# A gated mix of segment attention and a feed-forward network: row maxima from high halves in four 32-row tiles, and the network in one pass

## The chip, the cores and the metric

The kernel runs on one core of a Trainium2 chip. The metric is the device time of one execution in microseconds; the median of three runs of the kernel before is 552.74 us (552.01 to 553.68). The core has TensorE (PE, matmuls, results in PSUM), VectorE (DVE), ScalarE (ACT), GpSimd (POOL) and SyncE (SP), which here issues all DMAs. PSUM has eight banks of 128 x 512 floats.

## The reference

From the same x (2048 x 448) come an attention result a and a feed-forward result b; the output is g a + (1 - g) b, with g a sigmoid of x times a gate vector. The sequence falls into N = 4 segments of L = 512, with H = 16 heads of Dh = 28.

```python
logits = einsum("bhqd,bhkd->bhqk", qs, ks) * scale + mask     # causal, within a segment
a_dot = einsum("bhqk,bhkd->bhqd", softmax(logits), vs)
a_mem = (phi(qs) @ M) / (phi(qs) @ z + 1e-6)                  # memory of earlier segments
o = sigmoid(beta) * a_mem + (1 - sigmoid(beta)) * a_dot
M, z = M + phi(ks)^T vs, z + sum(phi(ks))
a = o @ wo
b = silu(x @ w1) @ w2                                         # 448 -> 1792 -> 448
```

Inputs are float32. The kernel reaches that accuracy with pairs of 16-bit numbers: every operand is split into a high and a low half (`halves`: one ScalarE copy, one subtraction), and a product is the sum of three matmuls: high by high, high by low and low by high.

## The kernel before, in words

**Stage one** (`project`) makes Q, K and V of every segment, the gates, and the memory part of attention. Q and K are made for a group of four heads at a time (112 of 128 rows; the 16 others carry a slice of the 14th block of w1, so that its x @ w1 comes along). With 4 segments and 4 groups there are 16 groups t. The halves of Q, K and V go out to DRAM and come back in another layout: a tile of `ring` holds for four heads 84 rows, the halves (high, low, high) of Q beside (high, high, low) of K, and two rows more for the negative row maximum.

**Row maxima** (`maxima`, L620): softmax wants a maximum for each row before the exponentials. For a group of heads TensorE multiplies the 84 rows of Q and K again, row block by row block (i = 0 to 3, with 128 (i+1) columns, causal), into banks "sc". For i = 0 a matmul with a mask (L640) goes ahead, and one VectorE instruction reduces four heads; the rest is masked and reduced by VectorE at once (L654). The maxima are transposed, split in halves, sent through DRAM and put into the two extra rows of `ring` as a term of the score product, lifted by 8 ln 2.

**Attention** (`attention`, L1160): for each head three score tiles, keys by queries (L1182), exponentials on ScalarE (L1187), two GpSimd instructions that zero what is not causal (L1190, L1193), the high half on ScalarE (L1199) and the low half in three GpSimd subtractions (L1203), then P times V with a column of ones for the denominators (L1216, into "cc") and the sum on VectorE (L1224). At the end of a group the result is scaled and stored to `o_scr`.

**The network** (`unit`, L1051) works in two passes over w1's 14 blocks of 128 columns: blocks 0 to 9 for all four segments, then 10 to 13. For a segment, each block gives a 128 x 512 tile of x @ w1 (11 matmuls by `product`, L540), the activation (ScalarE, VectorE, ScalarE, VectorE: L1063 to L1069), and the tile in halves in one of 12 buffers `ghl`. Then for each of four 128-token blocks the second product sums over the pass's blocks (three matmuls of 448 columns for each block, L1086). The first pass leaves partial sums in `p_scr` (`part`); the second takes them back. All blocks of w1 and w2 are loaded once in stage one to find their sizes, and again before their use; five blocks of w1 are converted at the end of stage one, the rest of the first pass's at the start of attention, the second pass's between the passes.

**The output** (`last_part`, L1280) belongs to the second pass: the attention result of a token block is loaded, the memory part added (GpSimd), split, transposed by DMA, multiplied by wo (11 matmuls of 448 columns), and added to both parts of the network's result in two VectorE instructions.

**What sets the order.** `Sched` is a planner that runs while the program is built: every piece of work is a task with an engine, a cost in microseconds, dependencies, buffers and a priority number; it walks in modelled time, gives each engine the task that can begin first and, among equals, that of the lowest priority, and so writes out a fixed order for every engine, SP's queue too. Attention's priorities are 10 per head (0 to 640), the first pass's are spread from -69 to 870. PSUM banks are rings: "mm" 4, "sc" 3, "cc" 1 after stage one. A task that takes a buffer waits until the one that many places earlier is used up. Constants at the top shift priorities of single kinds of work.

The line numbers named are those of the kernel before.

## Time and profile before

| | |
|---|---|
| median of 3 runs | 552.74 us (552.01 to 553.68) |
| profiled execution, its own time | 553.39 us |
| its span, first to last instruction | 551.7 us |
| mean granted TensorE clock | 0.984 |
| TensorE, VectorE, ScalarE, GpSimd busy | 534.8, 409.3, 391.8, 354.7 us |
| moved by DMA | 81.68 MB, mean 148 GB/s |

A busy share is a mean over stages. Matmuls are pipelined and the end of each is modelled, so that neighbours overlap in the record and the sum of durations is more than what the stream takes; the distance from one start to the next is what counts. A group of instructions shows its count, its busy time, the mean duration of one in ns, and the idle time of the engine just before them with the releaser. The chain of waits goes back from the last instruction to what released it each time.

### The profile page before, as it was taken

What the parts mean: (1) busy time and instruction counts of PE and PEld (TensorE: products, weight loads), DVE (VectorE), ACT (ScalarE), POOL (GpSimd) and SP (SyncE); (2) the same over time, 40 slices, a digit from 0 to 9 for tenths busy, and PEclk for the clock granted to TensorE, in tenths of its full rate; (3) what the DMA queues carried; (4) which work ended last, traced back from release to release, by engine and by line L of the source; (5) the groups of instructions that cost most, each with busy time, mean ns of one, the idle gap of its engine ahead of it and who ended that gap; (6) DMA issues with size and microseconds to landing.
All of it is one profiled execution on the core that took longest, in us unless ns stands there. A gap on an engine that the chain in (4) does not pass through costs nothing.

```text
span 551.7 us, 11563 instructions
## 1 busy us (share of the span) xinstructions
PE 534.8 (97%) x4009; PEld 294.7 (53%) x4009; DVE 409.3 (74%) x1074; ACT 391.8 (71%) x688; POOL 354.7 (64%) x519
## 2 busy tenths in 40 slices
PE   4699999999999999999999999999999999999997
...
PEclk8689999999999999999999999999999999999999
...
GB/s 276 205 175 227 203 236 233 225 226 166 170 233 162 146 100 137 87 42 80 121 102 102 58 98 124 121 103 112 100 18 53 138 49 152 219 241 212 225 160 83
DMA packets 89194, 81.68 MB, mean 148 GB/s; under 512 B 55176, under 2 KB 78856, under 8 KB 89136
## 3 DMA queue, kind: packets, MB, share of 16 engines
...
q14 instruction: 27, 0.22, 0.1%
...
## 4 chain that ended last, share of the span: by engine, by line
PE 89%; DVE 4%; DMA 4%; ACT 1%; issue 1%; SPq 0%; DVEq 0%; ACTq 0%
PE mm L540 31%; PE mm L1086 23%; PE sc L540 12%; PE sc L1182 6%; PE sc L644 6%; PE cc L1216 6%; DMA rawf<-in_w_dram 2%; PE cc L932 1%; DMA xraw<-in_x_dram 1%; PE cc L895 1%; DVE sizes L388 1%; DVE sc L654 1%; DMA v_scr<-vt 1%; PE sc L640 1%; PE cc L933 0%
## 5 line engine op out<-in xcount | busy, mean ns | idle before, releaser
L1203 POOL TENSOR_TENSOR phl<-pf,phl 128x384 f16<-128x384 f32 (+1 forms) x192 | 189.5, 1008 | 16.2 <-ACT phl L1199 16.2
L1086 PE MATMUL mm<-wb,ghl 128*128 128x448 f16 (+1 forms) x684 | 148.8, 349 | 0.0
L540 PE MATMUL mm<-xh,wa 128*128 128x512 f16 x572 | 141.4, 379 | 0.0
L1187 ACT ACTIVATE pf<-sc,es 128x512 f32<-128x512 f32 (+1 forms) x192 | 109.7, 623 | 19.8 <-PE sc L1182 18.6
L654 DVE CUSTOM_DVE_ANT_0 sc<-sc,mk 128x384 f32<-128x384 f32 (+1 forms) x192 | 104.8, 572 | 20.4 <-PE sc L644 19.1
L1086 PEld LDWEIGHTS <-ghl 128*128 128x128 f16 x684 | 65.0, 97 | 52.5 <-DVE ghl L508 0.3
L1199 ACT ACTIVATE phl<-pf 128x1280 f16<-128x1280 f32 x64 | 81.3, 1277 | 14.9 <-POOL pf L1193 14.9
L540 PEld LDWEIGHTS <-wa 128*128 128x128 f16 x572 | 53.6, 97 | 54.4 <-issue 1.4
L1182 PE MATMUL sc<-ring 86*128 86x512 f16 (+3 forms) x256 | 59.3, 299 | 0.4 <-ACT pf L1187 0.2
L644 PE MATMUL sc<-ring 84*128 84x128 f16 (+3 forms) x256 | 58.2, 299 | 0.1
L1224 DVE TENSOR_REDUCE oraw<-cc 128x116 f32<-128x232 f32 x64 | 25.3, 395 | 30.8 <-PE cc L1216 30.6
L1063 ACT ACTIVATE th<-mm,ths 128x512 f32<-128x512 f32 x52 | 35.8, 699 | 16.0 <-PE mm L540 15.8
L1216 PEld LDWEIGHTS <-phl 128*128 128x128 f16 x1280 | 41.9, 96 | 9.1
L540 PE MATMUL mm<-xh,wqs 128*128 128x512 f16 x176 | 44.5, 390 | 1.0 <-ACT wqs L516 0.7
L551 POOL TENSOR_TENSOR ol<-ol,ml 128x448 f32<-128x448 f32 x12 | 13.7, 1138 | 48.7 <-DMA ol<-o_scr 37.2
L1065 DVE SCALAR_TENSOR_TENSOR mm<-th,mm 128x512 f32<-128x512 f32 x52 | 35.7, 694 | 10.9 <-ACT th L1063 10.9
L1216 PE MATMUL cc<-vg,phl 128*128 128x29 f16 (+1 forms) x1280 | 43.6, 182 | 0.0
L540 PE MATMUL sc<-wvs,xh 128*128 128x450 f16 x176 | 39.9, 368 | 3.1 <-ACT wvs L516 2.1
L540 PE MATMUL mm<-xh,wks 128*128 128x512 f16 x176 | 42.1, 380 | 0.0
L1069 DVE SCALAR_TENSOR_TENSOR ghl<-mm,ghl 128x512 f16<-128x512 f32 x52 | 35.1, 683 | 5.6 <-ACT ghl L1067 5.2
L1182 PEld LDWEIGHTS <-ring 86*128 86x128 f16 x256 | 23.8, 97 | 22.0 <-issue 1.1
L1067 ACT ACTIVATE ghl<-mm 128x512 f16<-128x512 f32 x52 | 30.9, 604 | 6.5 <-DVE mm L1065 6.4
(165 smaller groups left out, 835.9 us busy)
## 6 DMA issues: line engine op xcount, KB each, us to landing
...
```

What stands on the lines that cost most here:

```text
L540: nc.tensor.matmul(ps(), *p[i], start=(i == 0), stop=(i == n - 1))
L644: nc.tensor.matmul(ps.v[:, u:u + n], rg.v[:KS, 0, hh, i * 128:(i + 1) * 128], rg.v[:KS, 1, hh, :n], start=(i > 0), stop=(i > 0 or j == 3), ...
L654: nc.vector.tensor_tensor_reduce(r, r, MK[:, L - n:], 1.0, NEG, OP.add, OP.max, mx.v[:, hh, i:i + 1])
L1063: e1 = sact(L, lambda ps=ps, th=th: nc.scalar.activation(th.v, ps.v, AF.Tanh, scale=ths[:, s:s + 1]), m, DER[s], takes=[th], uses=[ps], pr ...
L1065: e2 = dve(L, lambda ps=ps, th=th: nc.vector.scalar_tensor_tensor(ps.v, th.v, 1.0, ps.v, op0=OP.add, op1=OP.mult), e1, uses=[ps, th], prio=p0)
L1069: e4 = dve(L, lambda ps=ps, g=g: nc.vector.scalar_tensor_tensor(g.v[:, 1], ps.v, DOWN, g.v[:, 0], op0=OP.mult, op1=OP.subtract), e3, uses= ...
L1086: nc.tensor.matmul(ps.v[:, lo:hi], g.v[:, y, sl], w.v[:, z, lo:hi], start=(j == 0 and i == 0), stop=(j == len(fs) - 1 and i == 2))
L1182: nc.tensor.matmul(ps.v[:, e:e + w], rg.v[:KK, 1, hh, j * 128:(j + 1) * 128], rg.v[:KK, 0, hh, j * 128:], start=True, stop=True)
L1187: ex.append(sact(e, lambda b=b, ps=ps, pf=pf, e=e: nc.scalar.activation(pf.v[:, b, :e], ps.v[:, :e], AF.Exp, scale=es[:, s:s + 1]), m, *ex ...
L1199: hi = copy(1280, lambda hl=hl, flat=flat: nc.scalar.activation(hl.v[:, 0], flat(), AF.Copy), *mk, takes=[hl], uses=[pf], prio=p0 + 2)
L1203: low = pool(w - u, lambda hl=hl, flat=flat, u=u, w=w: nc.gpsimd.tensor_sub(hl.v[:, 1, u:w], flat()[:, u:w], hl.v[:, 0, u:w]), low, uses=[ ...
L1216: nc.tensor.matmul(p[:, i, :2 - z], hl.v[:, z, u:u + 128], vg.v[:, j, hh, :2 - z], start=(z == zs[0] and i == 0), stop=(z == zs[-1] and j ...
```

## The change

1. *Row maxima from the high halves alone, four heads at once.* The scratch tensors of Q and K become one per segment, stored in one DMA of 128 rows. Beside `ring`, a tile `hq` is loaded with the high halves of Q and K: head h lies in rows 32 h to 32 h + 27. Three steps of matmuls take four heads each, every head in its own 32 rows of the array and its own bank ("sc", "sc", "sc", "cc"); the planner treats a step as one task that takes four banks, costs it as one head's columns and a constant (`SWITCH`), and holds back other tasks for these banks when it is due. The matmul with the mask is gone, and VectorE masks and reduces every block of every head. The maximum of high halves is not the exact maximum; the lift becomes 6 ln 2.
2. *A guard.* The whole kernel becomes `mix`. After attention it checks that the reciprocals of all denominators lie between 1/60000 and 1/32 and sets a flag. At the end, if the flag is set, a second copy of the program runs with exact maxima.
3. *The network in one pass.* All 13 blocks of w1 and 14 of w2 are loaded once, measured and converted in place through rings of 14 and 15 buffers, which stay. `unit` takes a segment in two halves of 256 tokens: two blocks of w1 fill one bank of 512 columns with matmuls of 256; block 12 and the slice from Q and K are made for the whole segment. The second product sums over all 14 blocks. Partial sums of the network go through `p_scr` for 14 of 16 token blocks, and their outputs (`outcome`) are placed beside the attention of later segments; for the last two, the output product comes first and the network's result is added to it at the end.
4. *The start.* After 15 dummy matmuls, 16 more in eight tasks of the lowest priority. Most priorities, ring sizes and slacks have new numbers (attention still 10 per head, the network from -8 to 1048).

```diff
-LIFT = 8.0 * math.log(2.0)
+LIFT = 6.0 * math.log(2.0)
+DENS = (32.0, 60000.0)
...
-NA = 5
+NA = 14
+NBW = 15
 COLD = 5.0
 WARM = 15
+WARM2 = 8
...
+HW = 32
+QB = "sc", "sc", "sc", "cc"
+HOLD = -0.34
...
+        if t.rings and not t.wide:
+            for w in self.wide:
+                if w.prio < t.prio and any(r.n > 1 for r in w.rings & t.rings) and self.ready(w, "PE") < s + HOLD:
+                    return None
...
+FALL = True
...
+    args = x, wq, wk, wv, wo, beta, w1, w2, out
+    bad = ctx.enter_context(tc.tile_pool(name="bad", bufs=1)).tile([1, 1], I32, name="bad")
+    mix(tc, bad, *args)
+    if FALL:
+        with tc.If(tc.nc.values_load(bad[0:1, 0:1]) != 0):
+            mix(tc, None, *args)
...
+    qkscr = [dram(f"qk_scr{s}", (2, NG, 128, 2, L), F16) for s in range(NSEG)]
...
+    def get_w(j, f, r, d, prio):
+        ALL, n = slice(None), 4 if j == W1 else 1
+        w = Buf(WAR if j == W1 else WBR)
+        lo = [((ALL, slice(n, 2 * n)), (ALL,), (ALL, slice(0, n)))]
+        (WA if j == W1 else WB)[f] = w, halves(j, (ALL, slice(0, n)), lo, lambda: w.v, lambda: flat(r.v).rearrange("p (a b) -> p a b", a=n),
+                                               L if j == W1 else D, d, prio, takes=[w], uses=[r])
...
+        hq = None
+        if not exact:
+            hq = Buf(C["hq"])
+            hd = []
+            for j, st in ((0, QST[t]), (1, KST[t])):
+                hd.append(dma(131e3, lambda j=j: start(
+                    hq.v[:, j], qkscr[s][j, g].rearrange("(d h) z n -> h d z n", h=4)[:, :, 0]), st, *(hd[:1] or HDONE),
+                    takes=[] if hd else [hq], uses=[hq], prio=o - 70))
+            HDONE[:] = hd
+        early = o - 70 + (0 if exact else RING0)
+        rg = Buf(RG)
...
+        def masked(ps, hh, i, u):
+            r = ps.v[:, u:u + 128 * (i + 1)]
+            nc.vector.tensor_tensor_reduce(r, r, MK[:, L - 128 * (i + 1):], 1.0, NEG, OP.add, OP.max, mx.v[:, hh, i:i + 1])
...
+        for q, parts in enumerate(() if exact else (((3, 0),), ((2, 0), (0, 384)), ((1, 0),))):
+            banks = [Buf(BK[n]) for n in QB]
+            p0 = o - MAXO + 40 * q / 3
+
+            def go(parts=parts, banks=banks):
+                for i, u in parts:
+                    n = 128 * (i + 1)
+                    for hh in range(4):
+                        b = slice(HW * hh, HW * hh + DH)
+                        nc.tensor.matmul(banks[hh].v[:, u:u + n], hq.v[b, 0, i * 128:(i + 1) * 128], hq.v[b, 1, :n],
+                                         start=True, stop=True)
+            m = pe([x for i, u in parts for x in half(128 * (i + 1))], go, *hd, *MKS, takes=banks + [mx] * (q == 0), uses=[hq, mx], prio=p0)
+            m.costs["PE"] += SWITCH
+            for hh, ps in enumerate(banks):
+                cols = sum(128 * (i + 1) + 160 for i, u in parts) - 70
+
+                def red(parts=parts, ps=ps, hh=hh):
+                    for i, u in parts:
+                        masked(ps, hh, i, u)
+                reds.append(dve(cols, red, m, uses=[ps, mx], prio=p0))
...
+        for _ in range(WARM2):
+            pe(half(L, 2), lambda: [nc.tensor.matmul(
+                wb.v, maskb, maskb[:, None, :].to_broadcast([128, 4, 128]), start=True, stop=True) for _ in range(2)],
+                t_wb, uses=[wb], prio=500)
...
+            st = dma(262e3, lambda: start(qkscr[s][int(which == "k"), g], hl.v), hi, lo, uses=[hl], prio=prio)
...
+        got = []
+        for i in range(FREE + FB):
+            j, f = (W1, i) if i < FREE else (W2, i - FREE)
+            r, p = Buf(WAR if j == W1 else WBR), SZ + i * SZSTEP
+            if j == W1:
+                d = dma(262e3, lambda r=r, f=f: start(flat(r.v).rearrange("p (a b) -> p a b", a=4), w1[f]), WLOAD[-1], takes=[r], prio=p)
+            else:
+                d = dma(229e3, lambda r=r, f=f: start(flat(r.v), w2[f]), WLOAD[-1], takes=[r], prio=p)
+            total(j, lambda r=r: flat(r.v), L if j == W1 else D, d, uses=[r], prio=p)
+            got.append((j, f, r, d))
...
+        for j, f, r, d in got:
+            get_w(j, f, r, d, (WPRIO - WFP * (f < 4) if j == W1 else WBP) + 2 * f)
...
+    def gated(s, blocks, ring, prio):
+        ps, th, g = Buf(BK["mm"]), Buf(TH), Buf(ring)
+        p0 = prio(11 * L)
+        m, u = None, 0
+        for f, tok in blocks:
+            n = tok.stop - tok.start
             w, wd = WA[f]
-            m = product(lambda ps=ps: ps.v, lambda w=w: passes(w.v, X16[s]), L, p0, deps=wd + PREV,
-                        takes=[ps, g], uses=[w], kind=half)
-            e1 = sact(L, lambda ps=ps, th=th: nc.scalar.activation(th.v, ps.v, AF.Tanh, scale=ths[:, s:s + 1]), m, DER[s], takes=[th],
-                     uses=[ps], prio=p0)
-            e2 = dve(L, lambda ps=ps, th=th: nc.vector.scalar_tensor_tensor(
-                ps.v, th.v, 1.0, ps.v, op0=OP.add, op1=OP.mult), e1, uses=[ps, th], prio=p0)
-            e3 = act(L, lambda ps=ps, g=g: nc.scalar.activation(g.v[:, 0], ps.v, AF.Copy, scale=DOWN), e2,
-                     uses=[ps, g], prio=p0)
-            e4 = dve(L, lambda ps=ps, g=g: nc.vector.scalar_tensor_tensor(
-                g.v[:, 1], ps.v, DOWN, g.v[:, 0], op0=OP.mult, op1=OP.subtract), e3, uses=[ps, g], prio=p0)
-            gt[f] = g, [e3, e4]
-            t1[f] = m
+            m = product(lambda u=u, n=n: ps.v[:, u:u + n], lambda w=w, tok=tok: passes(w.v, X16[s][:, :, tok]), n, p0,
+                        deps=wd + PREV, takes=[] if m else [ps, g], uses=[w, ps, g], kind=half)
             PREV[:] = [m]
-        for tb in range(TB):
-            ps = Buf(BK["mm"])
-            p0 = prio(3 * len(fs) * D)
-            sl = slice(tb * 128, (tb + 1) * 128)
-            last, lasts = None, []
-            halves = [(0, D // 2), (D // 2, D)] if tail and tb == TB - 1 else [(0, D)]
-            for lo, hi in halves:
-                for j, f in enumerate(fs):
-                    g, w = gt[f][0], WB[f][0]
-
-                    def go(g=g, w=w, j=j, ps=ps, sl=sl, lo=lo, hi=hi):
-                        for i, (y, z) in enumerate(((0, 0), (0, 1), (1, 0))):
-                            nc.tensor.matmul(ps.v[:, lo:hi], g.v[:, y, sl], w.v[:, z, lo:hi], start=(j == 0 and i == 0),
-                                             stop=(j == len(fs) - 1 and i == 2))
-                    last = pe(half(hi - lo, 3), go, last or m, *([] if last else list(gate) + [PRE.get("b")]), *gt[f][1], *WB[f][1],
-                              takes=[ps] if last is None else [],
-                              uses=[ps, g, w], prio=p0)
-                    if lo == 0 and j == 0:
-                        PRE["b"] = last
-                    if tb == TB - 1:
-                        t2[f] = last
-                lasts.append((last, lo, hi))
-            finish(s, tb, ps, lasts, p0)
-        return t1, t2
+            u += n
+        e1 = sact(L, lambda: nc.scalar.activation(th.v, ps.v, AF.Tanh, scale=ths[:, s:s + 1]), m, DER[s], takes=[th],
+                  uses=[ps], prio=p0)
+        e2 = dve(L, lambda: nc.vector.scalar_tensor_tensor(ps.v, th.v, 1.0, ps.v, op0=OP.add, op1=OP.mult), e1,
+                 uses=[ps, th], prio=p0)
+        e3 = act(L, lambda: nc.scalar.activation(g.v[:, 0], ps.v, AF.Copy, scale=DOWN), e2, uses=[ps, g], prio=p0)
+        e4 = dve(L, lambda: nc.vector.scalar_tensor_tensor(g.v[:, 1], ps.v, DOWN, g.v[:, 0], op0=OP.mult, op1=OP.subtract), e3,
+                 uses=[ps, g], prio=p0)
+        return g, [e3, e4], m
...
+    def unit(s, prio, finish):
+        lone = {}
+        for hf in range(2):
+            gt = []
+            tok = slice(HALF * hf, HALF * (hf + 1))
+            for f in range(0, LONE, 2):
+                g, e, m = gated(s, [(f, tok), (f + 1, tok)], GTR, prio)
+                gt += [(f, g, 0, e), (f + 1, g, HALF, e)]
+            if hf == 0:
+                lone[FREE] = spare(s, prio(0), m)
+                g, e, m = gated(s, [(LONE, slice(0, L))], GLR, prio)
+                lone[LONE] = g, e
+            gt += [(f, g, HALF * hf, e) for f, (g, e) in sorted(lone.items())]
+            for tb in (2 * hf, 2 * hf + 1):
+                ps = Buf(BK["mm"])
+                p0 = prio(3 * FB * D)
+                last, lasts = None, []
+                end = s == NSEG - 1 and tb == TB - 1
+                for lo, hi in [(0, D // 2), (D // 2, D)] if end else [(0, D)]:
+                    for j, (f, g, u, e) in enumerate(gt):
+                        w = WB[f][0]
+                        u += 128 * (tb % 2)
+
+                        def go(g=g, w=w, j=j, u=u, ps=ps, lo=lo, hi=hi):
+                            for i, (y, z) in enumerate(((0, 0), (0, 1), (1, 0))):
+                                nc.tensor.matmul(ps.v[:, lo:hi], g.v[:, y, u:u + 128], w.v[:, z, lo:hi], start=(j == 0 and i == 0),
+                                                 stop=(j == FB - 1 and i == 2))
+                        last = pe(half(hi - lo, 3), go, last or m, *([] if last else [PRE.get("b")]), *e, *WB[f][1],
+                                  takes=[ps] if last is None else [], uses=[ps, g, w], prio=p0)
+                        if lo == 0 and j == 0:
+                            PRE["b"] = last
+                    lasts.append((last, lo, hi))
+                finish(s, tb, ps, lasts, p0)
...
+        ra, ps = rall.rearrange("p t h i -> p (t h i)"), Buf(BK["cc"])
+
+        def sums():
+            nc.vector.tensor_scalar(MK[:, :NT * 4 * TB], ra, 1.0 / DENS[1], None, op0=OP.is_ge)
+            nc.vector.scalar_tensor_tensor(MK[:, :NT * 4 * TB], ra, 1.0 / DENS[0], MK[:, :NT * 4 * TB], op0=OP.is_le, op1=OP.mult)
+            nc.vector.tensor_reduce(fine, MK[:, :NT * 4 * TB], axis=AX.X, op=OP.min)
+        f = dve(900, sums, *RALL, prio=FHI + 300)
+        f = pe(ful(128), lambda: nc.tensor.transpose(ps.v[:1, :128], fine, ident), f, takes=[ps], prio=FHI + 300)
+
+        def verdict():
+            nc.vector.tensor_reduce(fine[:1], ps.v[:1, :128], axis=AX.X, op=OP.min)
+            nc.vector.tensor_scalar(fine[:1], fine[:1], -1.0, 1.0, op0=OP.mult, op1=OP.add)
+            nc.vector.tensor_copy(bad, fine[:1])
+        dve(500, verdict, f, uses=[ps], prio=FHI + 300)
...
+            e2 = dve(D, lambda: nc.vector.scalar_tensor_tensor(y.v, pw.v[:, :D], gas[:, k:k + 1], pl.v, op0=OP.mult, op1=OP.add), m,
+                     d2, PRE.get("a"), takes=[y], uses=[pw, pl], prio=prio)
+            dma(229e3, lambda: start(out[k * 128:(k + 1) * 128, :], y.v), e2, uses=[y], prio=prio)
+        else:
+            ps, lasts, p1 = late
+            e2 = act(D + 110, lambda: nc.scalar.activation(y.v, pw.v[:, :D], AF.Copy, scale=gas[:, k:k + 1]), m, PRE.get("a"),
+                     takes=[y], uses=[pw], prio=prio)
+            for last, lo, hi in lasts:
+                e3 = dve(hi - lo, lambda lo=lo, hi=hi: nc.vector.scalar_tensor_tensor(
+                    y.v[:, lo:hi], ps.v[:, lo:hi], ogs[:, k:k + 1], y.v[:, lo:hi], op0=OP.mult, op1=OP.add), e2, last,
+                    uses=[y, ps], prio=p1)
+                dma(512.0 * (hi - lo), lambda lo=lo, hi=hi: start(out[k * 128:(k + 1) * 128, lo:hi], y.v[:, lo:hi]), e3,
+                    uses=[y], prio=p1)
...
+    def finish(s, tb, ps, lasts, prio):
+        if s == NSEG - 1 and tb >= 2:
+            outcome(s, tb, prio - WOQ, (ps, lasts, prio))
+        else:
+            part(s, tb, ps, lasts, prio)
+            FINAL.append((s, tb))
+
+    FINAL, LATE_END = [], []
+    prio = spread(FLO, FHI, NSEG * (FREE * 11 * L + FB * TB * 3 * D))
+    for s in range(NSEG - 1):
+        unit(s, prio, finish)
+    for s, tb in FINAL:
+        outcome(s, tb, 160.0 * (s + 1) + WOP + 8 * tb)
+    FINAL.clear()
+    unit(NSEG - 1, prio, lambda s, tb, *a: LATE_END.append((s, tb, *a)) if tb >= 2 else finish(s, tb, *a))
+    for s, tb in FINAL:
+        outcome(s, tb, 160.0 * (s + 1) + WOP + 8 * tb)
+    for a in LATE_END:
+        finish(*a)
```

348 lines of the change are left out of this document (139 added, 209 removed).

## The prediction

> **What bounds the kernel now.** I read the page's busy shares and slices first, then its chain of waits, then busy time by stretches.
>
> ```profile
> span 551.7 us, 11563 instructions
> PE 534.8 (97%) x4009; PEld 294.7 (53%) x4009; DVE 409.3 (74%) x1074; ACT 391.8 (71%) x688; POOL 354.7 (64%) x519
> ...
> PE   4699999999999999999999999999999999999997
> ...
> PEclk8689999999999999999999999999999999999999
> ...
> PE 89%; DVE 4%; DMA 4%; ACT 1%; issue 1%; SPq 0%; DVEq 0%; ACTq 0%
> ```
>
> TensorE is busy in every slice but the first two and the last, and 89% of the chain that ends last is TensorE. But a busy mark is not a full rate, since the ends of matmuls are modelled, so I look for the rate in the stretches.
>
> ```profile
> 0.00:14.00 14.00, 6.32 (x18) 2.23 (x19) 8.51 (x29) 2.45 (x3) 4.11 (x26) 0.81 0.81 277
> 14.00:28.00 14.00, 9.43 (x37) 3.94 (x36) 12.25 (x38) 7.52 (x18) 0.28 (x1) 0.71 0.63 206
> 28.00:42.00 14.00, 13.50 (x57) 5.65 (x58) 12.26 (x38) 11.62 (x32) 9.97 (x17) 0.88 0.53 177
> 42.00:56.00 14.00, 14.00 (x67) 6.41 (x66) 13.63 (x38) 12.52 (x26) 4.82 (x10) 1.00 0.80 218
> ...
> 490.00:504.00 14.00, 14.00 (x75) 7.08 (x73) 5.57 (x11) 1.37 (x3) 2.26 (x2) 1.00 0.83 209
> ...
> 165.00:457.00 292.00, 291.55 (x2682) 166.98 (x2681) 206.93 (x597) 246.99 (x389) 255.59 (x355) 1.00 0.35 98
> ```
>
> The columns after the length are TensorE, weight loads, VectorE, ScalarE and GpSimd, then the granted clock and the DMA share. From 490 to 504 us TensorE does almost only 448-column matmuls, 75 in 14 us: 187 ns each, or 0.417 ns per column. It is at that rate from 42 us on, so from there to the end the kernel is as long as its matmul columns. Only the first 42 us (12.8 us idle, and a lower clock) and the tail hold anything else. A microsecond of matmul taken away after 42 us is therefore worth a microsecond, if the other engines follow: between 165 and 457 us, where attention runs, GpSimd is busy 256 of 292 us and ScalarE 247, so the room there is about 12%.
>
> **The row maxima: what goes.** The old pass multiplies 84 rows (three products of high and low halves stacked) for one head at a time; these are its groups by shape.
>
> ```profile
> L644 PE MATMUL sc<-ring 84*128 84x512 f16 x64 | 24.3, 380 | 0.1
> L644 PE MATMUL sc<-ring 84*128 84x384 f16 x64 | 20.9, 326 | 0.0
> ...
> L644 PE MATMUL sc<-ring 84*128 84x256 f16 x64 | 10.4, 272 | 0.0
> ...
> L644 PE MATMUL sc<-ring 84*128 84x128 f16 x64 | 6.2, 218 | 0.0
> L640 PE MATMUL sc<-maskb,identb 128*128 128x512 bf16 x16 | 6.1, 379 | 0.0
> ```
>
> Their busy times include the modelled ends. What they take from the stream is the distance to the next start, in the timeline of TensorE:
>
> ```profile
> 229.41 0.33 PE L644 MATMUL sc<-ring 84*128 84x384 f16 x1
> 229.57 0.81 PE L540 MATMUL mm<-xh,wa 128*128 128x512 f16 x3
> ...
> 238.62 0.38 PE L640 MATMUL sc<-maskb,identb 128*128 128x512 bf16 x1
> 238.83 0.39 PE L644 MATMUL sc<-ring 84*128 84x128 f16 x4
> 239.06 0.38 PE L1182 MATMUL sc<-ring 86*128 86x512 f16 x1
> ...
> 242.74 0.38 PE L644 MATMUL sc<-ring 84*128 84x256 f16 x2
> 242.96 0.81 PE L540 MATMUL mm<-xh,wa 128*128 128x512 f16 x3
> ```
>
> A 512-column matmul takes 0.21 us, a 384 one 0.16, four of 128 0.23, two of 256 0.22. One group of four heads takes the mask matmul 0.21, then 0.23, 2 x 0.22, 4 x 0.163 and 4 x 0.216: 2.40 us; sixteen groups make 38.4 us, which the change removes.
>
> **What comes in its place.** Per group of heads three steps: four matmuls of 512 columns; four of 384 and four of 128; four of 256. Each head has its own 32 rows of the array and its own PSUM bank. If the four heads run together, only one head's columns count: 1280 x 0.417 ns and four starts, 0.54 us. No row shows two matmuls at once. But the array goes from full height to a few rows and back in this trace already, in the scale matmuls of one or two rows:
>
> ```profile
> 127.86 1.46 PE L540 MATMUL mm<-xh,wqs 128*128 128x512 f16 x6
> 129.25 0.17 PE L427 MATMUL cc<-diag,oneb 2*128 2x2 bf16 x1
> 129.35 1.25 PE L540 MATMUL mm<-xh,wqs 128*128 128x512 f16 x5
> ```
>
> Six full matmuls should take 1.30 us, and the stream goes on 1.49 us after they began: 0.19 us for a matmul of two columns, nearly all of it getting in and out. The ends for a step's overhead are nothing (8.7 us in all for the new maxima) and 0.33 us, twice the 0.16 us by which a 512-column matmul's modelled 0.38 us is longer than its distance to the next (24.5 us in all). I take 0.19, the nearest row: 0.54 + 3 x 0.19 = 1.11 us per group, 17.8 us in all. **Gain 20.6 us; between 13.9 and 29.7 if the heads overlap.** If they do not, four times the columns at 0.33 give 50.5 us, a loss of 12.1.
>
> The Trainium skill, "TensorE: Matmul & The Clock Gate" (Measured speedup vs the span model), gives 3.07 times, not four, for four row tiles of 512 columns. By it the column part would be 0.71 us, and the forecast 2.6 us later. Its page "TensorEngine Tiling (Array Packing)" (Key Properties) states that a change of tiling mode drains TensorE, which speaks against scattering 48 such steps among full-height matmuls; a full drain both ways, 0.33 us by the rows above, would put the forecast 6.7 us later. The 0.19 us row shows a cost of that kind, but smaller.
>
> **VectorE and the banks.** The mask matmul goes, so the 128-column blocks too are masked and reduced on VectorE, head by head.
>
> ```profile
> L654 DVE CUSTOM_DVE_ANT_0 sc<-sc,mk 128x512 f32<-128x512 f32 x64 | 45.2, 706 | 12.8 <-PE sc L644 12.7
> L654 DVE CUSTOM_DVE_ANT_0 sc<-sc,mk 128x384 f32<-128x384 f32 x64 | 37.1, 579 | 4.5 <-PE sc L644 4.5
> ...
> L654 DVE CUSTOM_DVE_ANT_0 sc<-sc,mk 128x256 f32<-128x256 f32 x64 | 27.0, 431 | 3.0 <-PE sc L644 2.0
> L654 DVE DVE_READ_ACCUMULATOR2_ANT mx<- 128x1 f32 x192 | 26.9, 140 | 0.0
> L1224 DVE TENSOR_REDUCE oraw<-cc 128x116 f32<-128x232 f32 x64 | 25.3, 395 | 30.8 <-PE cc L1216 30.6
> ...
> L649 DVE TENSOR_REDUCE mx<-sc 128x4 f32<-128x512 f32 x16 | 10.9, 680 | 1.6 <-PE sc L644 1.6
> ```
>
> A 128-column reduction has no row; going down by another 0.14 us from the 0.43 of 256 gives 0.29, with 0.14 for reading the result: 64 x 0.43 = 27.5 us come, 10.9 go. VectorE was busy 207 of 292 us in attention, so 16.6 us more lie beside TensorE's other work: 0. Uncovered they would cost all 16.6. What is queued behind a step is the score matmuls and P times V: a step takes all three "sc" banks and the one "cc" bank at once, and they come back as VectorE works through them. TensorE has the network in the four "mm" banks meanwhile. I cost this at 0 and make it a rival.
>
> **The network in one pass.** The same columns, but 1056 matmuls of 256 columns stand for 528 of 512 (4 segments, 2 halves, 6 pairs, 2 x 11). Two of 256 took 0.22 us, one of 512 0.216: **+1.5 us**, between 0 and 5 by the 0.01 us resolution. Second products, output products and their columns stay. The second load of 27 weight blocks goes away; the chain has 4% of DMA, at places where TensorE worked on, so 0. The 22 conversions that stood at the start of attention and between the passes move ahead of the first unit:
>
> ```profile
> L508 DVE SCALAR_TENSOR_TENSOR wa<-rawf,up,wa 128x512 f16<-128x512 f32 x12 | 10.9, 917 | 1.9 <-ACT wa L516 1.9
> ...
> L516 ACT ACTIVATE wa<-rawf,up 128x512 f16<-128x512 f32 x13 | 9.2, 726 | 3.3 <-DMA rawf<-in_w_dram 3.0 <-DMA v_scr<-vt 0.3
> ```
>
> They go through a ring with one spare slot, so one block's steps follow one another: 0.73 + 0.92 = 1.64 us and two hand-overs. The stage before has 13.6 of 14 us of VectorE taken, GpSimd under half. Each first product of a pair gives TensorE 22 x 0.11 = 2.4 us while two blocks take 3.3. I cost it at 0 because conversions are allowed to begin during the projections, and keep it as a rival. The extra loads of high halves (two for each group, on SP's queue ahead of the score operands' loads) displace two small stores per group there: 0.
>
> **The start.** Sixteen dummy matmuls at the lowest priority fill waits in the projections. If the clock were 1.00 throughout, the busy time at 0.71 and 0.88 would shrink by 9.43 x 0.29 + 13.50 x 0.12 = 4.4 us. I take half, **-2.2** (0 to -4.4), since weights and VectorE (12.3 of 14 us) also hold that stretch. The changed order of loads and size reductions there may cost or bring a few microseconds.
>
> **The guard.** At the end every engine reads a flag and branches past the second copy of the program. No row shows a branch. The last vector instruction and the end of the span give the nearest latency:
>
> ```profile
> 548.06 0.81 DVE L1297 SCALAR_TENSOR_TENSOR y<-mm,ogs,ya 128x224 f32<-128x224 f32 x2 [0.47 <-PE mm L1086]
> ```
>
> From 548.9 to 551.7 us the last output lands: 2.8 us. A branch costs 0 if it hides behind that, 5.6 if two such latencies follow it; I take **+2.8**, one. The flag itself is ready long before, when the last denominators are.
>
> **Sum.** 551.7 - 20.6 - 2.2 + 1.5 + 2.8 = 533.2 us of span. The profiled execution took 553.39, 1.7 more than its span, and the median is 552.74, 0.65 less: 534.2, **forecast 534 us**. With every bound at its good end 551.7 - 29.7 - 4.4 = 517.6, or 518.6 by the median's measure; with the bad ends of overlapping heads, 551.7 - 13.9 + 5 + 5.6 = 548.4, or 549.4.
>
> **Rivals.**
> *The cheap case*: no overhead at the steps and a warm start, 519 to 526 us. For it: the network keeps TensorE supplied. Against: the 0.19 us row.
> *The conversions starve TensorE*: 0.9 us for each of six pairs, and as much again for the second products, are 11 us, of which other work covers part: 541 to 551 us.
> *The four heads do not run together* (the change does not do what it says): 534 + 20.6 + 12.1 = 567 us; with the middle overhead, 562. Against it: rows and banks are separate.
> *The banks become the bound*, slower than before. Attention's pace now is in the first and last exponential, and the way from the last one to its stored output:
>
> ```profile
> L1187 ACT ACTIVATE pf<-sc,es x192: 462/681/811, 176.9 to 449.9; 128x512 f32<-128x512 f32 x128, 128x256 f32<-128x256 f32 x64
> ...
> L324 SPq DMA_DIRECT2D o_scr<-ob x16: 371/384/388, 211.4 to 464.2; - x16
> ...
> 236.80 0.68 PE L1216 MATMUL cc<-vg,phl 128*128 128x29 f16 x20
> 237.32 1.24 PE L540 MATMUL mm<-xh,wa 128*128 128x512 f16 x5
> ```
>
> 273 us for sixteen groups, 17.1 each. The single "cc" bank, drained last, is held for 4 x (0.85 + 1.15 + 0.57) = 10.3 us of reductions, 1.1 us of the steps and 4 x (0.52 + 0.40) = 3.7 us of P times V with its sum: 15.1 us, before some 14 hand-overs. At 0.2 us each this is 17.9, near the pace of now. It decides only when attention ends so late that nothing covers the last segment's way out: 14 us to the store and some 16 for load, transposition and four output products (2.1 us each). 176.9 + 16 T + 30 passes 551.7 at T = 21.6 us, that is hand-overs and waits for four free banks of 0.46 us each. At T = 22.5 the time is 567 + 1 = 568 us.
> *The guard trips* and the general copy runs: over 1000 us. With the reference's inputs the lifted denominators lie between 64 and 22059, inside 32 to 60000, so this is excluded but for a fault.
>
> **How the numbers follow.** Forecast (527 to 540) 0.55, cheap case 0.18, conversions 0.11, heads in series 0.07, banks 0.08, guard 0.01. A measurement of this kernel tells no change from one below 0.3%, 551.1 to 554.4 us. Of the conversions' case and the forecast's upper edge 0.05 falls there. So faster 0.79 (0.55 + 0.18 + 0.06), same 0.05, slower 0.16. The range takes in the first three cases, 0.84: 518 to 551 us.
>
> **What would show it.** Score matmuls of 28 rows should start in fours within a few hundredths of a microsecond, and the next full-height matmul some 0.4 us after a 512-column step began; if it starts 0.9 us later, they run in series. TensorE's count should stay saturated from about 40 us to the end at 75 matmuls of 448 columns per 14 us. Gaps at 150 to 200 us with conversions as releaser mean the conversions; score matmuls waiting on the vector reductions, and exponentials that end after 490 us, mean the banks. A clock of 1.00 from 14 us on confirms the fillers. The span's end more than 3 us past the last output store shows the guard's price. A time above 551 us, or TensorE below 95% busy after 50 us, would prove the picture of a kernel as long as its columns wrong.

## The result, and the profile after

The changed kernel takes 640.63 us in the median of four runs (639.45 to 646.77), the kernel before, run beside it, 552.38 us. The ratio is 1.161 with a 95% interval of 1.155 to 1.168: 16% slower, where 534 us (518 to 551) had been forecast. The profiled execution took 646.77 us, the longest of the four; its span is 644.6 us.

These are the lines of its page that answer to those shown of before: busy times, TensorE in 40 slices, its granted clock, and the chain of waits by engine and by line.

```profile
span 644.6 us, 12703 instructions
PE 551.2 (86%) x4568; PEld 339.5 (53%) x4568; DVE 409.6 (64%) x1173; ACT 397.1 (62%) x688; POOL 371.3 (58%) x521
...
PE   5899988999757596967979889779699986999994
...
PEclk9799998999977787979879889899799996999998
...
PE 56%; DMA 17%; DVE 8%; SPq 6%; POOL 5%; issue 4%; ACT 2%; POOLq 0%; DVEq 0%; ACTq 0%
PE mm L583 20%; PE mm L1144 16%; PE sc L583 8%; SPq L364 6%; DMA ring<-m_scr 6%; PE sc L1224 6%; DMA ring<-qk_scr 5%; PE cc L1259 4%; DMA big<-in_wo_dram 2%; PE sc L698 1%; DMA xraw<-in_x_dram 1%; POOL am L995 1%; DVE xh L551 1%; DMA ol<-o_scr 1%; POOL phq L886 1%
```

The chain was 89% TensorE and 4% DMA. Now TensorE has 56%, DMA 17%, and SP's queue, which had 0%, has 6%. Two loads carry most of the DMA share, both into `ring`: the score operands (`qk_scr`, 5%) and the two small rows of maxima (`m_scr`, 6%). No other engine became the bound: VectorE, ScalarE and GpSimd are busy for about as long as before in a span that is 93 us longer.

The same by stretches, with TensorE, weight loads, VectorE, ScalarE, GpSimd, the granted clock and the DMA share:

```profile
42.00:154.00 112.00, 105.06 (x607) 57.91 (x605) 99.97 (x259) 86.72 (x186) 62.04 (x90) 0.98 0.69 179
154.00:182.00 28.00, 20.11 (x159) 15.19 (x158) 21.69 (x41) 18.78 (x34) 17.63 (x20) 0.93 0.40 126
182.00:574.00 392.00, 331.19 (x3123) 209.01 (x3120) 223.22 (x712) 238.57 (x369) 246.76 (x337) 0.90 0.31 87
574.00:644.60 70.60, 62.33 (x553) 43.45 (x551) 29.20 (x56) 27.32 (x42) 30.78 (x39) 0.96 0.59 143
```

The loss lies in attention, 182 to 574 us. TensorE stands 392 - 331.2 = 60.8 us there, and by an estimate the clock of 0.90 lengthens its 331 us of work by some 33 us more (a tenth of it). The DMA engines are on the mean less than a third busy (0.31): as a whole they are not short of bandwidth.

What TensorE and ScalarE wait for (line waited for: us in total, times, longest):

```profile
ACT pf L1229 <- PE sc L1224: 99.3, 61, 8.9
...
PE sc L1224 <- DMA ring<-m_scr: 26.1, 5, 8.3
...
PE sc L1224 <- DMA ring<-qk_scr: 12.3, 4, 4.2
```

One such wait in the timeline of all engines, for one group of heads:

```profile
241.19 0.33 SPq L364 DMA_DIRECT2D m_scr<-mhl  x1
...
244.93 0.67 SPq L364 DMA_DIRECT2D ring<-m_scr  x1
...
245.66 6.33 SPq L364 DMA_DIRECT2D ring<-qk_scr  x3
...
249.06 0.68 DVE L1112 SCALAR_TENSOR_TENSOR mm<-th,mm 128x512 f32<-128x512 f32 x1
...
252.54 0.59 PE L1224 MATMUL sc<-ring 86*128 86x512 f16 x1 [5.55 <-DMA ring<-m_scr]
```

The load of two rows, 8 KB, is issued at 244.93 and TensorE can use it at 252.54; in the chain of waits the transfer has 7.36 us:

```profile
244.93 7.36 DMA ring<-m_scr
...
269.85 9.47 DMA ring<-m_scr
```

The first score matmul of a group stands at the head of TensorE's queue, and behind it the network's matmuls, which have what they need: TensorE stands 5.55 us, and by 249.8 us the other engines have run dry too. Meanwhile three loads of score operands for a later group hold SP for 6.33 us (0.88, 0.65 and 4.72 us, the last a load of 28 rows), and what is queued behind them waits too. The issues by tile, duration in ns (minimum, median, maximum); before:

```profile
L324 SPq DMA_DIRECT2D ring<-q_scr x32: 307/372/607, 40.2 to 384.5; - x32
L324 SPq DMA_DIRECT2D ring<-k_scr x32: 375/385/622, 53.1 to 385.3; - x32
L324 SPq DMA_DIRECT2D ring<-m_scr x16: 228/240/269, 106.9 to 436.4; - x16
```

and after:

```profile
L364 SPq DMA_DIRECT2D ring<-qk_scr x64: 646/793/5709, 76.7 to 532.8; - x64
L364 SPq DMA_DIRECT2D ring<-m_scr x16: 252/618/1542, 102.2 to 574.6; - x16
```

The bytes and the number of these loads are what they were. What differs is the order of their source in DRAM. Before, `q_scr` and `k_scr` were stored so that a load of 56 rows (28 high, 28 low) read 56 rows of 4 KB, rows outermost. In the new scratch tensor, (d h) z n, high and low halves z lie side by side, and the same load reads the halves outermost, a dimension of size 2, then 112 pieces of 1 KB in each. The load of `hq` has the four heads outermost.

The Trainium skill, "DMA: Bandwidth & Descriptors" (Why a DMA increments its semaphore by 16 and not by 1), states that a DMA runs on the largest number of engines, up to 16, that divides the slowest dimension of both its access patterns, and that for SP these are the lowest-numbered ones. By it the load of 56 rows ran on 14 engines before and on 2 now, the small load of two rows stands on the same two behind it, and the DMA share stays low while both are slow. The rows are as this would have them. Which engines carried a load no run here shows; for how many, the traces have a sign.

The end of a load is recorded as writes to a semaphore. Before, each 56-row load ended with 15 of them, in the changed kernel with 3; a load of `hq`, four outermost, has 5. If one write goes with each engine and one more stands for those left out, that is 14, 2 and 4, the numbers of the rule. From its issue to the last write, the sixteen loads of two rows took at most 3.4 us before, and in the changed kernel eleven of them took 5.9 to 9.5; the 56-row loads took 3.0 (Q) and 3.9 (K) us in the median before and 9.8 after.

### The profile page after: what moved, and what is told of

It is laid out like the page before. It is cut to its first block, busy times and chain, and to the rows that moved or that the text cites. A ratio compares the mean times of both kernels' runs of the same rounds, so it can differ in the third digit from the quotient of the medians.

```text
span 644.6 us, 12703 instructions
## 1 busy us (share of the span) xinstructions
PE 551.2 (86%) x4568; PEld 339.5 (53%) x4568; DVE 409.6 (64%) x1173; ACT 397.1 (62%) x688; POOL 371.3 (58%) x521
## 4 chain that ended last, share of the span: by engine, by line
PE 56%; DMA 17%; DVE 8%; SPq 6%; POOL 5%; issue 4%; ACT 2%; POOLq 0%; DVEq 0%; ACTq 0%
PE mm L583 20%; PE mm L1144 16%; PE sc L583 8%; SPq L364 6%; DMA ring<-m_scr 6%; PE sc L1224 6%; DMA ring<-qk_scr 5%; PE cc L1259 4%; DMA big<-in_wo_dram 2%; PE sc L698 1%; DMA xraw<-in_x_dram 1%; POOL am L995 1%; DVE xh L551 1%; DMA ol<-o_scr 1%; POOL phq L886 1%
## 5 line engine op out<-in xcount | busy, mean ns | idle before, releaser
L583 PE MATMUL mm<-xh,wa 128*128 128x256 f16 (+1 forms) x1100 | 153.1, 288 | 1.0 <-DVE amr L986 1.0
L1144 PE MATMUL mm<-wb,ghl 128*128 128x448 f16 (+1 forms) x612 | 136.3, 362 | 0.0
L679 DVE CUSTOM_DVE_ANT_0 sc<-sc,mk 128x128 f32<-128x128 f32 (+1 forms) x192 | 91.0, 514 | 55.3 <-PE cc L698 51.3
L583 PEld LDWEIGHTS <-wa 128*128 128x128 f16 x1100 | 107.1, 102 | 28.2 <-issue 6.7
L1224 PE MATMUL sc<-ring 86*128 86x512 f16 (+3 forms) x256 | 66.0, 329 | 58.3 <-DMA ring<-m_scr 26.1
L1144 PEld LDWEIGHTS <-ghl 128*128 128x128 f16 x612 | 59.0, 102 | 47.8 <-issue 12.3
L1232 POOL TENSOR_SCALAR_AFFINE_SELECT pf<-pf 128x256 f32<-128x256 f32 x64 | 27.3, 427 | 75.5 <-ACT pf L1229 75.3
L679 DVE DVE_READ_ACCUMULATOR2_ANT mx<- 128x1 f32 x256 | 36.2, 141 | 0.0
L583 PE MATMUL sc<-wos,oT 128*128 128x448 f16 x176 | 35.8, 352 | 0.0
L1115 DVE SCALAR_TENSOR_TENSOR ghl<-mm,ghl 128x512 f16<-128x512 f32 x48 | 32.4, 682 | 4.0 <-ACT ghl L1114 3.7
```

The costliest lines, as they stand in the source:

```text
L583: nc.tensor.matmul(ps(), *p[i], start=(i == 0), stop=(i == n - 1))
L679: nc.vector.tensor_tensor_reduce(r, r, MK[:, L - 128 * (i + 1):], 1.0, NEG, OP.add, OP.max, mx.v[:, hh, i:i + 1])
L1115: e4 = dve(L, lambda: nc.vector.scalar_tensor_tensor(g.v[:, 1], ps.v, DOWN, g.v[:, 0], op0=OP.mult, op1=OP.subtract), e3, uses=[ps, g], pr ...
L1144: nc.tensor.matmul(ps.v[:, lo:hi], g.v[:, y, u:u + 128], w.v[:, z, lo:hi], start=(j == 0 and i == 0), stop=(j == FB - 1 and i == 2))
L1224: nc.tensor.matmul(ps.v[:, e:e + w], rg.v[:KK, 1, hh, j * 128:(j + 1) * 128], rg.v[:KK, 0, hh, j * 128:], start=True, stop=True)
```

## The experiments

### Is it the shape of the loads?

Theory A: the outermost dimension of 2 in the load of score operands. Theory B: the pieces of 1 KB in place of 4 KB. Theory C: the loads are issued too late or in a worse place of SP's queue. The first three edits below leave the order of instructions on the four other engines as it was; in the fourth the planner wrote another.

**Two loads in place of one**, in the changed kernel: each half is a load of its own, with 28 rows outermost.

```diff
-start(rg.v[lo:lo + 2 * DH, j], src)
+[start(rg.v[lo + DH * z:lo + DH * z + DH, j], src[z]) for z in (0, 1)]
```

> The changed kernel with each 56-row load of score operands (source outermost: the two halves) issued as two loads of 28 rows, one per half; the same 1 KB pieces, the same place in the queue, the same planned order. Theory A (a load whose source counts its two halves outermost goes to few DMA engines, the small load of the row maxima queues behind it there, and TensorE, in order, waits): the waits of the score matmuls on DMA (26 + 12 us on TensorE, 26 us on its weight loads) fall under 10 us, the granted clock rises to 0.97 or more, and the time falls to 525 to 560 us. Theory B (the loads are slow because they come in 1 KB pieces instead of 4 KB) expects 620 us or more, since the pieces stay and two issues are added per group. Theory C (the loads are issued too late in the planned order, with three ring buffers instead of four) expects no change beyond 2%.

Measured: 553.72 us, ratio to before 1.0023 (1.0004 to 1.0043). One line of loads brings back 87 us of the 88. Each of the two loads now ends with 15 writes, and the loads of two rows take at most 2.4 us. The issues into `ring`:

```profile
L364 SPq DMA_DIRECT2D ring<-qk_scr x96: 787/800/1295, 75.4 to 446.9; - x96
L364 SPq DMA_DIRECT2D ring<-m_scr x16: 256/282/368, 94.6 to 481.2; - x16
```

The longest issue falls from 5.7 to 1.3 us, and the small load's from 1.5 to 0.4. By stretches:

```profile
42.00:154.00 112.00, 109.41 (x646) 61.60 (x645) 105.85 (x266) 91.28 (x197) 68.46 (x98) 1.00 0.70 187
154.00:196.00 42.00, 32.19 (x215) 19.89 (x213) 32.86 (x91) 23.64 (x39) 21.65 (x24) 0.92 0.60 152
196.00:541.00 345.00, 344.78 (x3561) 232.27 (x3560) 232.38 (x700) 253.32 (x393) 267.38 (x362) 1.00 0.43 115
```

From 196 to 541 us TensorE is full again at a clock of 1.00, the state that the forecast took for the whole. Of what is missing against the forecast, the largest part now lies ahead of 196 us, where TensorE stands 2.6 and 9.8 us.

**The same dimension put into the kernel before**: its scratch tensors get four unused rows in each half, so that halves and rows no longer merge into one dimension of 56. The pieces stay 4 KB, and nothing else changes.

```diff
-    qscr = [dram(f"q_scr{t}", (2, DH, 4, L), F16) for t in range(NT)]
-    kscr = [dram(f"k_scr{t}", (2, DH, 4, L), F16) for t in range(NT)]
+    qscr = [dram(f"q_scr{t}", (2, 32, 4, L), F16) for t in range(NT)]
+    kscr = [dram(f"k_scr{t}", (2, 32, 4, L), F16) for t in range(NT)]
...
-                rg.v[lo:lo + 2 * DH, j], scr.rearrange("z d h n -> (z d) h n")), st, *(rs[:1] or RDONE),
+                rg.v[lo:lo + 2 * DH, j], scr[:, :DH]), st, *(rs[:1] or RDONE),
```

> The kernel before, with the scratch of Q and K padded from 28 to 32 rows per half, so that the 56-row load's source counts the two halves outermost; the 28 pieces per half stay 4 KB, everything else the same. Theory A: this alone slows the kernel before, to 565 us or more (32 such loads, and the row maxima's small load behind them), though less than in the changed kernel since there the loads stand earlier and a fourth ring buffer waits. Theories B and C expect the time of before within 1%.

Measured: 615.53 us, ratio 1.112 (1.108 to 1.117). Its chain of waits and one of its waits show the same two loads, in a kernel that has nothing else of the change; its 56-row loads end with 3 writes, as in the changed kernel, and six of its sixteen loads of two rows take 6.8 to 7.8 us:

```profile
PE 67%; DMA 18%; DVE 8%; ACT 2%; POOL 1%; issue 1%; SPq 1%; DVEq 0%
PE mm L540 23%; PE mm L1086 18%; PE sc L540 9%; DMA ring<-m_scr 7%; PE sc L1182 6%; DMA rawf<-in_w_dram 5%; PE cc L1216 5%; PE sc L644 4%; DMA ring<-k_scr 3%; DMA xraw<-in_x_dram 1%; SPq L324 1%; DVE sc L654 1%; DVE sizes L388 1%; PE cc L932 1%; DVE stg L807 1%
```

```profile
PE sc L1182 <- DMA ring<-m_scr: 22.2, 6, 4.2
```

**Larger pieces, still two outermost**: in the changed kernel the halves lie apart in DRAM, with 4 KB for each row of a head group.

```diff
-    qkscr = [dram(f"qk_scr{s}", (2, NG, 128, 2, L), F16) for s in range(NSEG)]
+    qkscr = [dram(f"qk_scr{s}", (2, NG, 2, 128, L), F16) for s in range(NSEG)]
...
-            src = qkscr[s][j, g].rearrange("(d h) z n -> z d h n", h=4)[:, :DH]
+            src = qkscr[s][j, g].rearrange("z (d h) n -> z d h n", h=4)[:, :DH]
```

> The changed kernel with its scratch ordered half by half, so that a row of the score operands is one piece of 4 KB again as before the change; the 56-row load's source still counts the two halves outermost. Theory A: 600 us or more. Theory B: 525 to 560 us. Theory C: no change beyond 2%.

Measured: 633.28 us, ratio 1.146 (1.141 to 1.151). Only 7 us come back: the size of the pieces is a small part, theory B falls. The long issues are nearly gone in this run (for loads into `ring` one of 3.1 us, all others under 1.5), while eleven loads of two rows still take 5.7 to 8.1 us. So what costs is for the most part the time to the landing, and not SP held at the issue.

**Earlier loads**: the changed kernel with `RING0`, the later place of these loads, at nothing.

```diff
-RING0 = 37.94
+RING0 = 0.0
```

> The changed kernel with the score operands' loads 38 priority units earlier (RING0 = 0), as early as before the change. Theory C: under 590 us. Theories A and B: the loads stay as slow, 610 to 660 us.

Measured: 652.47 us, ratio 1.181 (1.173 to 1.188), no better and rather worse. The order is another here, so this run alone would not settle theory C; it falls by the first run, where the loads keep their place in the queue and the time comes back. Theory A is shown from both sides: the dimension of 2 taken away alone gives the 16% back, put in alone it costs 11%.

### What is the change worth without it?

**All loads spread**: the scratch tensor is laid out as half, head, row; `hq` reads 128 rows outermost, `ring` 28, and the slices of the 14th block have a tensor of their own.

```diff
-    qkscr = [dram(f"qk_scr{s}", (2, NG, 128, 2, L), F16) for s in range(NSEG)]
+    qkscr = [dram(f"qk_scr{s}", (2, NG, 2, 4, HW, L), F16) for s in range(NSEG)]
+    hscr = [dram(f"h_scr{s}", (2 * NG, 16, 2, L), F16) for s in range(NSEG)]
```

> The changed kernel with every load of Q and K spread: scratch ordered half, head, row; 28-row loads for the score operands, the high halves in loads whose source counts 128 rows outermost (4 in the run with 28-row loads alone), the spare rows in a scratch of their own. There the first load of high halves took 7.0 us from 164.8 us on and TensorE stood 4.9 us for it. Theory A (what is left of that gap is the same cause): the wait for high halves goes below 1 us, TensorE is idle less than 7 us between 154 and 196 us (10 us there), 542 to 549 us. Theory D (what is left is the order of SP's queue and VectorE's backlog at the change of stages): 550 to 556 us.

Measured: 551.59 us, ratio 0.9991 (0.9974 to 1.0007). The load of `hq`, which now ends with 16 writes, was good for some 2 us. TensorE's wait for it fell from 4.9 to 1.5 us, but other waits came: from 42 to 196 us TensorE stands 12.1 us, where it stood 12.4. The rest of the gap to the forecast is not in the shape of these loads.

**Without the guard**: the same with `FALL = False`, so that no second copy of the program is there.

> As the run with every load spread, without the branch and the second copy of the program; the flag is still computed, nothing acts on it. The span ended 6.5 us after the last vector instruction in the run with 28-row loads, 2.8 us before the change. Guard theory: 3 to 5 us less than with the guard. Rival (the branch hides behind the last store): within 1.5 us.

Measured: 547.82 us, ratio 0.9924 (0.9903 to 0.9945). The guard costs 551.59 - 547.82 = 3.8 us. The last vector instruction with the guard, in an execution of this span,

```profile
span 551.9 us, 12875 instructions
...
544.84 0.81 DVE L1346 SCALAR_TENSOR_TENSOR big<-mm,ogs,big 128x224 f32<-128x224 f32 x2 [1.50 <-ACT big L1343]
```

and without it:

```profile
span 545.3 us, 12850 instructions
...
541.71 0.81 DVE L1346 SCALAR_TENSOR_TENSOR big<-mm,ogs,big 128x224 f32<-128x224 f32 x2 [1.50 <-ACT big L1343]
```

From its end to the end of the span it is 6.3 us with the guard and 2.8 without. This version is 0.8% faster than the kernel before, with an output that is the same as long as the denominators stay in their bounds; it lacks what catches the other case.

**The old maxima in it**: the version without guard, made with the exact maxima of the general path, head by head from 84 rows.

```diff
-    mix(tc, bad, *args)
+    mix(tc, None, *args)
```

> The network in one pass with the exact maxima of the general copy (84 rows, one head at a time, no mask matmul), loads spread, without guard. 16 matmuls per group, 5120 columns at 0.417 ns and their starts, 2.17 us against 0.88: 21 us of TensorE more. Theory G: 12 to 21 us more than the run without guard. Rival H (the steps of four banks cost elsewhere what they save): within 6 us of it, or less.

Measured: 570.44 us, ratio 1.0325 (1.0290 to 1.0361), so the new maxima are worth 570.44 - 547.82 = 22.6 us there. The order written out differs between the two, so a few of these may be the planner's. The steps in TensorE's timeline, in the version without guard:

```profile
442.51 0.34 PE L699 MATMUL sc<-hq 28*128 28x384 f16 x3
442.52 0.33 PE L699 MATMUL cc<-hq 28*128 28x384 f16 x1
...
442.84 2.25 PE L584 MATMUL mm<-xh,wa 128*128 128x256 f16 x19
444.92 0.38 PE L1225 MATMUL sc<-ring 86*128 86x512 f16 x1
...
448.07 1.36 PE L584 MATMUL mm<-xh,wa 128*128 128x256 f16 x11
449.37 0.28 PE L699 MATMUL sc<-hq 28*128 28x256 f16 x3
...
449.59 1.38 PE L584 MATMUL mm<-xh,wa 128*128 128x256 f16 x11
450.80 0.38 PE L1225 MATMUL sc<-ring 86*128 86x512 f16 x1
...
453.82 0.39 PE L699 MATMUL sc<-hq 28*128 28x512 f16 x3
...
454.15 1.69 PE L584 MATMUL mm<-xh,wa 128*128 128x256 f16 x8
```

Four heads start within 0.01 us of each other, and the next matmul starts 0.33 us after a step of 384 and 128 columns began, 0.22 after one of 256, 0.33 after one of 512. That is the way out alone; there is a way in too. Eleven matmuls of 256 columns take 1.21 us up to a score matmul (449.59 to 450.80) and 1.30 up to a step (448.07 to 449.37). Over all steps the matmul ahead of one lasts 0.096 us longer than elsewhere in the median (0.205 in place of 0.109 for 256 columns, 0.285 in place of 0.189 for 448). A group takes 0.33 + 0.33 + 0.22 + 3 x 0.096 = 1.16 us in place of 2.40, sixteen groups 19.8 us less. The 0.88 us and 24 us in two of the expectations leave the way in out.

The exact maxima of the general path have no matmul with the mask and take 2.22 us per group in the rows of this run, so that 16 x (2.22 - 1.16) = 17 us of the 22.6 stand in TensorE's stream. The rest is not accounted for.

**The new maxima alone**, in the kernel before, without a guard, with the spread loads and the network in its two passes:

```diff
-        plan = [(0, [0, 1, 2, 3]), (1, [0, 1]), (1, [2, 3])] + [(i, [h]) for h in range(4) for i in (2, 3)]
-        for q, (i, hs) in enumerate(plan):
...
+        for q, parts in enumerate(() if False else (((3, 0),), ((2, 0), (0, 384)), ((1, 0),))):
+            banks = [Buf(BK[n]) for n in QB]
```

> The kernel before with the new maxima alone: the planner's tasks of four banks, four heads at once from high halves, loads spread as in the run with every load spread; the network keeps its two passes. No guard. The steps took 0.33, 0.33 and 0.22 us with 28-row loads, 0.88 us per group against 2.40: 24 us of TensorE. Theory G (the kernel is as long as its matmul columns): 526 to 534 us. Rival H (steps of four banks and 16.6 us more of VectorE hold attention back): 543 to 556 us, with TensorE idle in attention.

Measured: 600.55 us, ratio 1.087 (1.083 to 1.091). By stretches:

```profile
434.00:462.00 28.00, 21.45 (x182) 9.99 (x181) 21.83 (x73) 21.31 (x34) 27.34 (x37) 0.82 0.29 78
462.00:490.00 28.00, 18.88 (x188) 9.65 (x186) 18.24 (x60) 22.98 (x36) 23.98 (x35) 0.53 0.14 37
490.00:518.00 28.00, 16.13 (x166) 9.94 (x167) 3.31 (x9) 12.59 (x18) 24.08 (x33) 0.50 0.07 19
```

Until 434 us TensorE is full. Then the first pass of the network is used up, the second waits for all of attention, and attention alone, with GpSimd 27 of 28 us busy at first, cannot fill TensorE; its clock goes to 0.50. The saving on TensorE is not the whole of it: attention itself became slower. Its exponentials run from 182.0 to 505.2 us, 20.2 us for each group against 17.1 before, while TensorE was still full up to 434. Whether the steps that take four banks slow it, as rival H says, or the order, which the planner wrote with the old priorities and the new costs, was not tested apart. Shown is that in this kernel the new maxima did not gain by themselves, and that with the network in one pass, which gives TensorE work up to the end of attention, they did.

### What is left ahead of 196 us?

The version without guard, by stretches:

```profile
42.00:126.00 84.00, 78.00 (x450) 42.32 (x449) 74.75 (x190) 67.05 (x149) 43.85 (x64) 1.00 0.79 212
126.00:196.00 70.00, 64.24 (x441) 39.84 (x441) 67.05 (x178) 50.83 (x93) 47.31 (x60) 1.00 0.54 156
196.00:541.00 345.00, 345.00 (x3542) 231.96 (x3540) 232.37 (x698) 251.54 (x388) 267.32 (x361) 1.00 0.43 115
```

TensorE stands 6.0 and 5.8 us in the first two, where it stood 0.2 before; VectorE is busy 67 of 70 us in the second. All runs of this part are variants of this version, and so without the guard.

**Conversions off VectorE**: the low halves of the 27 weight blocks are not computed, GpSimd writes zeros.

```diff
+        if j in (W1, W2):
+            o = lo[0][0]
+            return [h, pool(n, lambda: nc.gpsimd.memset(dst()[o], 0.0), h, uses=tuple(takes) + tuple(uses), prio=prio)]
```

> The kernel without the guard and with the spread loads (547.82 us) in which the low halves of the 27 blocks of w1 and w2 are not computed: GpSimd writes zeros in their place. Some 19 us of VectorE's work go (27 times about 0.72 us), nearly all of it between 126 and 196 us, where VectorE is now busy 13.3 to 13.9 of every 14 us and TensorE stands 5.9 us. Theory E (the conversions, on a VectorE that is full there, leave TensorE without work): TensorE stands 2 us or less in that stretch, and the time falls by 3 to 6 us, to 542 to 545. Rival F (the change of stage itself: stores and loads on SP's queue, the banks that the first steps of maxima need, the order of the work): TensorE stands as long as before, within 1.5 us, and the time stays at 546.5 to 549.

Measured: 558.80 us, ratio 1.0119 (1.0099 to 1.0138), slower with less to do: the planner wrote another order, the high halves' copies on ScalarE came closer together (137 to 168 us, in place of 138 to 180), and TensorE stood behind ScalarE instead (9.2 us for the memory's operands). Inconclusive.

**Another bank**: a step takes a bank of "mm" in place of "cc".

```diff
-QB = "sc", "sc", "sc", "cc"
+QB = "sc", "sc", "sc", "mm"
```

> The kernel without the guard and with the spread loads (547.82 us) in which a step of the new maxima takes three sc banks and one of the four mm banks in place of the single cc bank. Theory H (the steps that fall into stage one hold the cc bank, so that the memory's matmuls and the measurement of sizes wait for VectorE there): the 4.4 us that the memory's matmuls wait between 56 and 126 us fall to under 2 and the time by 2 to 4 us, to 544 to 546. Rival I (VectorE is late there whatever bank it drains, and the network now loses one of its four banks to each step): the time is the same or up to 6 us longer, 547 to 554.

Measured: 675.56 us, ratio 1.224 (1.222 to 1.227). Theory H falls; rival I had the direction, but the time is far beyond its 554 us. TensorE stands all through attention:

```profile
196.00:532.00 336.00, 282.68 (x2550) 171.88 (x2550) 201.57 (x659) 214.50 (x330) 243.58 (x333) 0.83 0.34 91
```

The planner holds other tasks back from banks that a due step needs, where a ring has more than one (`HOLD` in the diff); with an "mm" bank among them it holds back the network too. That this makes the 128 us is an argument from the code; the order is another, and no run takes the hold away.

**The conversions of w2 later**, and **no fillers** at the start:

```diff
-WBP = 60.47
+WBP = 150.0
```

> The kernel without the guard and with the spread loads (547.82 us) in which the conversions of w2 have the priority number 150 in place of 60.47, so that they come after those of w1. Theory J (at the change of stage ScalarE and VectorE spend time on blocks of w2 that no second product needs yet, and the first products stand for blocks of w1): TensorE's idle time between 126 and 196 us falls from 5.9 us to under 3, its clock stays at 1.00, and the time is 543.5 to 546.5. Rival K (the same work only comes later, and a second product then waits for it with all four mm banks full of first products): as much or more idle time between 168 and 240 us, time 548 to 556.

```diff
-WARM2 = 8
+WARM2 = 0
```

> The kernel without the guard and with the spread loads (547.82 us) without the 16 added dummy matmuls of the start. Theory L (as predicted, the fillers raise the clock of the first 42 us, and a faster clock there is worth some 2 us): clock about 0.8 and 0.7 in the first two stretches of 14 us, 0.9 in the third, time 549 to 551.5. Rival M (what sets that stretch is the loads and the measurement of sizes on VectorE, which do not follow TensorE's clock): the clock falls as said and the time stays within 1 us, 547 to 548.8.

Measured: 564.50 us, ratio 1.022 (1.019 to 1.026), and 579.68 us, ratio 1.050 (1.048 to 1.053). Eight tasks of the lowest priority fewer, and the kernel is 32 us slower: the planner's order is another on every engine, and TensorE stands 26 us between 42 and 196 us. As tests of conversions and of the clock both are inconclusive; what they show is that a new order moves this kernel by 17 to 32 us. So the last two runs keep the planner's costs, and with them the order, and make only the instruction cheap.

**Conversions made cheap in their place**:

```diff
-                rest(e, dst()[o], src()[i], s[o[0]], dst()[f])
+                e.memset(dst()[o], 0.0) if j in (W1, W2) else rest(e, dst()[o], src()[i], s[o[0]], dst()[f])
```

> The kernel without the guard and with the spread loads (547.82 us), every instruction in its place, but the low halves of the 27 blocks of w1 and w2 are set to zero by a memset on the engine and at the place where they were computed; the planner's costs stay, so the order written out stays. The run that gave this work to GpSimd had another order, so it did not settle the question. Theory E (conversions on a full VectorE leave TensorE without work at the change of stage): with VectorE relieved of 5 to 15 us between 126 and 196 us TensorE stands 3 us or less there in place of 5.9, and the time is 542.5 to 546. Rival F (loads, stores and banks at the change of stage): within 1 us of the time before, 546.8 to 548.8.

Measured: 547.35 us, ratio 0.9907 (0.9876 to 0.9938).

```profile
126.00:196.00 70.00, 66.60 (x453) 41.39 (x452) 60.45 (x181) 52.36 (x97) 35.56 (x57) 1.00 0.59 167
```

VectorE has 6.6 us less, and TensorE stands 3.4 us in place of 5.8. The time is that of the version without guard within the spread of both, so the 2.4 us do not show in it. The conversions are behind part of the idle time, and they are not what keeps the time up.

**Fillers of one column**, in their place:

```diff
-                wb.v, maskb, maskb[:, None, :].to_broadcast([128, 4, 128]), start=True, stop=True) for _ in range(2)],
+                wb.v[:, :1], maskb, maskb[:, :1], start=True, stop=True) for _ in range(2)],
                 t_wb, uses=[wb], prio=500)
```

> The kernel without the guard and with the spread loads (547.82 us), every instruction in its place, but each of the 16 added dummy matmuls has one column in place of 512. In the run without them the order written out was another on every engine, so that its 32 us say nothing of the fillers themselves. Theory L (the fillers raise the clock, worth some 2 us, as predicted): clock 0.8 to 0.95 in the first 14 us, 0.7 to 0.76 from 14 to 28, below 1.00 from 28 to 42, time 549 to 551. Rival M (loads and sizes set that stretch): time 547 to 548.8, whatever the clock is.

Measured: 547.51 us, ratio 0.9916 (0.9890 to 0.9941), the same time. With fillers of one column, and with whole ones:

```profile
0.00:42.00 42.00, 30.41 (x144) 13.29 (x145) 37.02 (x113) 27.21 (x63) 14.03 (x39) 0.88 0.78 261
```

```profile
0.00:42.00 42.00, 33.93 (x138) 14.30 (x139) 35.78 (x108) 25.96 (x60) 14.09 (x38) 0.92 0.75 251
```

What is worth nothing is the length of the fillers: sixteen matmuls of one column give the time of sixteen of 512, so theory L's gain of 2 us from them falls. The clock moved by only 0.04, from 0.92 to 0.88, and what a start at the 0.80 of the kernel before would cost this version no run shows.

## Why the prediction was wrong, point by point

**The step that failed: the loads, costed at 0.** The prediction said of the added loads of high halves that they displace two small stores per group on SP's queue, and of the new layout of Q and K nothing. It counted the loads and never how each reads its source. The load of score operands has the same bytes, but its outermost dimension fell from 56 to 2, and that made 87 us of the 107 between the forecast of 534 and the result. Nothing in the profile of before could show it; the access pattern in the diff could. No rival had a slower load in it. The forecast's own tests told the case at once: a time above 551 us, TensorE below 95% busy after 50 us.

**The maxima: right, in mechanism and in size.** The four heads run at the same time, as said. Predicted were 1.11 us per group and a gain of 20.6 us; the rows give 1.16 and 19.8. A step of 512 columns takes 0.33 + 0.096 us, 0.21 more than one head's columns; steps of 256, and of 384 and 128, have the same 0.21. The 0.19 read off a matmul of two columns was the right row: it too has 0.09 us on the way in (129.25 in place of 129.16) and 0.10 on the way out.

**The network's 256-column matmuls: right.** Nineteen in a row, from 442.84 to 444.92 us, take 0.1095 us each, and 905 of them between 200 and 540 us that no step follows 0.1094. Before, 462 of 512 columns took 0.2168 each, so it is 1056 x (0.1094 - 0.1084), some 1 us, where 1.5 were taken.

**VectorE costed at 0, and the conversions costed at 0: wrong by 11.3 us together, in stage one and at the change of stage only.** From 196 us on the cover held: TensorE is full with VectorE busy 67% of the time. Ahead of it TensorE stands 11.8 us, where before stood 0.5 us from 42 us on. The prediction named the full VectorE of that stretch and let it pass. Emptying the conversions takes 2.4 us of this away; the rest is many short waits, none over 1.7 us. Of the 11.8 us, 8.7 end with an instruction of VectorE. Which of them comes first was not settled.

**The start: no gain from the fillers.** The clock of the first 42 us rose from 0.80 to 0.92, but it is 0.76 from 14 to 28 us, where 1.00 from 14 us on was named as the sign, and the version with fillers of one column is as fast. The 2.2 us taken for them do not show. Without the guard the forecast's span is 533.2 - 2.8 = 530.4 us and the measured one 545.3, 14.9 more. Of this 11.3 is the idle time and 0.8 the maxima, and the 256-column matmuls came out 0.4 cheaper. The second products add nothing: apart from those ahead of a step they take 0.190 us each, as before. Of the 3.2 us left, 2.2 can be the start's gain that did not come; the rest was not traced.

**The guard: right in kind**, 3.8 us against 2.8, inside its 0 to 5.6. It did not trip.

**The banks: not the bound, but nearer than said.** From the first to the last exponential, after and without guard:

```profile
L1229 ACT ACTIVATE pf<-sc,es x192: 449/680/691, 187.2 to 591.1; 128x512 f32<-128x512 f32 x128, 128x256 f32<-128x256 f32 x64
```

```profile
L1230 ACT ACTIVATE pf<-sc,es x192: 449/680/691, 180.8 to 495.8; 128x512 f32<-128x512 f32 x128, 128x256 f32<-128x256 f32 x64
```

The changed kernel needs 25.2 us per group, past the 21.6 from which attention decides, but by its loads. With the loads spread it needs 19.7, more than the estimate of 17.9 and still below 21.6. The exponentials end at 495.8 us, past the 490 that the prediction named as a sign of the banks, but TensorE is full to the end of attention, so nothing is lost by it there. That such a case can be dear is seen in two runs, 128 us with a bank of "mm" and 48 with the new maxima alone; in both the order is another too, so neither is the price of the banks by itself.

**Two slips in the sums.** Two matmuls of 256 at 0.22 us for one of 512 at 0.216 make 528 x 0.004 = 2.1 us, not 1.5. Heads in series with the middle overhead come to 560 us, not 562. Neither bears on the outcome.
